# Which half of the array opens an item: fixed, or whichever is free

## The chip, the core and the metric

The kernel runs on one core of a Trainium2 chip. The time is device microseconds of one execution; what is compared is the median of several. TensorE (PE in the profile) multiplies, VectorE (DVE), ScalarE (ACT) and GpSimd (POOL) do the rest, and SyncE (SP) issues nearly all DMA transfers.

## The reference

Everything is float32, with 2048 tokens and a width of 512. The normalized input feeds two branches, and their results are multiplied.

```
xn = layernorm(x)
qkv = xn @ wqkv                       # 32 heads of 16
p = softmax(q k^T / 4, masked)        # each query sees the 256 latest keys
s = (p v) @ wo                        # 512 x 512
h = silu(xn @ w_gate) * (xn @ w_up)   # 512 x 1792 each
g = silu(h @ w_down)                  # 1792 x 512
out = x + s * g
```

## The kernel before

**Precision.** Matmuls run on float32r, a format that keeps fewer bits than float32. Each operand is therefore split into a high part (ACT copies it to float32r) and a low part (the difference, by POOL for weights and hidden activations, by DVE for others), and each product is three matmuls: high by high, high by low, low by high (`PAIRS`).

**Two halves.** PE is used as two arrays of 64 rows, `r` = 0 (lower, partitions 0 to 63) and 1 (upper, partitions 64 to 127). They work at the same time. A contraction over 128 rows is one matmul in each half, and both add into the same PSUM bank, but not at the same time: one half puts its whole share of the bank down first (it *opens* the item), then the other adds its own (it *closes* it). Between the two stands a handover, a DVE copy of one column (`ho`) on which the closing half waits. In this kernel the lower half always opens and the upper always closes, at least `LAG` = 7 matmuls later while the lower has work (`ready`).

**Units and items.** A unit is a block of weights and the work on it, an item one PSUM bank of output. Tokens are taken in four chunks of 512. `Proj` (profile name a) makes q and k of two groups of four heads, `Values` (vp) makes v, `GateUp` (g and u) a block of 128 hidden columns, `Down` (d) a quarter of the down product for 256 columns, `Wo` (s) the output projection for 256 columns. All have two items here. `dense_order` lists the units, `stream` their items. Four PSUM banks (`pf0` to `pf3`) serve the items, four others (`pr`) attention.

**Weights.** Unit n's lower half needs rows 0 to 63 of its weights at one time, and its upper half needs the others later. So blocks are shifted: block n holds the lower rows of unit n and the upper rows of unit n−1 (`block`, `units_of`). `w_fetch` loads a block by two DMAs of 64 partitions into one of two raw buffers (`wr`), `w_split` splits it on ACT (`wh`, line 429) and POOL (`wl`, line 434) into one of three pairs of buffers. Where the two units of a block differ in width, a piece of 64 partitions is split by itself. A block's buffers are free once the lower half has ended its unit and the upper the one before (`unit_end`).

**Attention** is laid between the dense matmuls. For each of 32 units of four heads (8 per chunk) PE makes the scores once for their row maxima (b, line 970; DVE reduces them into `m`), transposes the maxima (`mt`), ACT negates them (`ms`), and a DMA writes them as an extra row of q (`q<-ms`). Then PE makes the scores again with the maximum subtracted (c, line 1124), ACT takes the exponential into `p` (line 1085), POOL masks the diagonal blocks, and PE multiplies by v (pv, line 1161). q and k pass through DRAM (`qkd`): `Proj.done` stores them and `load_qk` loads them into the layout that attention needs.

**The order.** The program is written by a planner that runs while it is built. It keeps a clock for each half and each engine with costs in microseconds, and decides by these which half issues its next matmul (`next_mm`), what each engine's queue holds (`do`, `pump`) and when a DMA is issued (`dma`). On the chip each engine then takes its queue strictly in that order. Two of its assumptions matter below: `qk_at`, when q and k of an attention unit have landed, and `ms_at`, when the maxima have landed in q.

Of the kernel before, what the change touches and what calls it, by code (L numbers as in the profile page):

```python
# [41 lines left out]
LAG = 7  # L42
# [13 lines left out]
def tile_window_attention_swiglu_gate(  # L56
# [305 lines left out]
    def block(n, r):  # L362
        return n + r if n else 0

    class Unit:
# [3 lines left out]
        def wts(self, r):  # L369
            return wtile[block(self.n, r)]  # L370
# [10 lines left out]
    def units_of(j):  # L381
        return weighted.get(j), weighted.get(j - 1 if j else 0) if j != 1 else None

    def w_fetch(j):
        lo, up = units_of(j)
        if lo is None and up is None:
            return
        parts = [(r, u) for r, u in ((0, lo), (1, up)) if u is not None]
        box = []

        def go(r, u):
            if not box:
                if j == 2:
                    box.append(pers.tile([P, 1024], F32, name="wr2", tag=f"hr{NHID - 1}", bufs=1))
                else:
                    box.append(sb(f"wr{j}", [P, 1024], F32, "wr", 2))
            move(box[0][half(r), : u.width], u.src[half(r)])

        def then(t, last):
            if last:  # L400
                landed[j] = (t, box[0])
                w_split(j)

        for n, (r, u) in enumerate(parts):
            dma(now[0], lambda r=r, u=u: go(r, u), lambda t, n=n: then(t, n == len(parts) - 1),
                slack=1.0, kb=256 if j > 2 else 200)

    wpart = {}

    def w_split(j):  # L410
        if j not in landed or (j >= 3 and j - 3 not in ended_unit):
            return
        t, raw = landed.pop(j)
        t = max(t, ended_unit.get(j - 3, 0.0))
        w = [u.width if u else 0 for u in units_of(j)]
        hi, lo = [], []
        both = min(w)
# [6 lines left out]
        def high(pr, a, b):  # L424
# [4 lines left out]
            nc.scalar.activation(hi[0][pr, a:b], raw[pr, a:b], AF.Copy)  # L429

        def low(pr, a, b):
            if j == 0 and a == 0:
                nc.gpsimd.tensor_copy(spare, xt[0, list(normed)[-1][1]][:, :1])
            nc.gpsimd.tensor_tensor(lo[0][pr, a:b], raw[pr, a:b], f32(hi[0][pr, a:b]), op=ALU.subtract)  # L434
# [9 lines left out]
        def after_high(t, pr, a, b, sl):  # L444
            wpart[j, a, 0] = t
            do("G", t, 0.17 + 0.0021 * (b - a), lambda: low(pr, a, b), lambda t: done(t, a), sl, lambda: len(normed) >= 4)

        for n, (pr, a, b) in enumerate(cuts):
            sl = (0.0 if j >= 3 else 0.2) + 0.3 * n
            if j == n == 0:  # L450
                sl = -3.0
            do("S", t, 0.13 + 0.00078 * (b - a), lambda pr=pr, a=a, b=b: high(pr, a, b),
               lambda t, pr=pr, a=a, b=b, sl=sl: after_high(t, pr, a, b, sl), sl)

    half_ended = set()
# [56 lines left out]
    class Stationary(Unit):  # L514
# [6 lines left out]
        def inputs(self, i):  # L521
            if self.c == 0 and self.n == 0 and i == 0:
# [3 lines left out]
        def mms(self, i, r, pb):  # L526
            w = [t.rearrange("p (a k n) -> p a k n", a=2, k=KC) for t in self.wts(r)]
            xs = xn[self.c % 2]
            if self.c == 0 and self.n == 0 and i == 0:
                for a, b in ((0, 0), (1, 0), (0, 1)):  # L530
                    for part in range(2):
                        n = slice(256 * part, 256 * part + 256)
                        for k in range(KC):
                            def go(first, last, k=k, a=a, b=b, n=n):
                                return mm(pb[:, n], w[a][half(r), i, k, :], xs[b][half(r), k, n], first, last)
                            yield 256, go, lambda k=k, a=a, b=b, part=part: latest(
                                [(xlow if b else xhigh).get((k, part)), wpart.get((0, 0, a))]
# [116 lines left out]
    class Moving(Unit):  # L654
# [4 lines left out]
        def mms(self, i, r, pb):  # L659
            w = [t[:, : self.width].rearrange("p (k n) -> p k n", n=256) for t in self.wts(r)]  # L660
            for t in range(2):
# [833 lines left out]
```

## Time and profile before

| | us |
|---|---|
| median of 3 runs (868.84, 870.20, 873.62) | 870.2 |
| the profiled execution | 871.9 |
| its span, first to last instruction | 870.1 |
| PE busy | 856.9 |
| POOL busy | 606.2 |
| ACT busy | 505.3 |
| DVE busy | 484.0 |

The profile was taken of one execution, and its span is 1.8 us shorter than that execution's time. Busy times are unions: PE counts as busy when either half works. In the lists, a row of the timeline gives the start and the length in microseconds, the engine, the line, the operation, the names written and read, the shape and a count of rows merged into it; brackets give the idle time before it and what ended it. PEld are weight loads of PE, and a name with q (SPq, ACTq) is that engine's instruction queue. A matmul's shape, 64*128 64x512, is the rows and columns of its tile of the array, and then the moving operand.

### The profile page before, as it was taken

How to read it: one execution, taken by the hardware profiler on the slowest of the kernel's cores; microseconds unless marked ns; L12 is line 12 of the kernel's file. 1: busy time of each engine (PE TensorE's matmuls, PEld its weight loads, DVE VectorE, ACT ScalarE, POOL GpSimd, SP SyncE). 2: the span in 40 equal slices, each digit the busy share in tenths (PEclk: the TensorE clock that was granted, in tenths of full speed). 3: DMA queues.
4: the chain of work that ended last, by engine and by line, in shares of the span. 5: the costliest groups of instructions: out<-in, count | busy, mean ns of one | idle time of the engine just before them, and what ended most of it. 6: DMA issues, size and time to landing. Idle time of an engine off the chain costs nothing.

```text
span 870.1 us, 29847 instructions
## 1 busy us (share of the span) xinstructions
PE 856.9 (98%) x11960; PEld 790.0 (91%) x11960; DVE 484.0 (56%) x1627; ACT 505.3 (58%) x1074; POOL 606.2 (70%) x648
## 2 busy tenths in 40 slices
PE   9999999999999999999999999999999999999997
PEld 8799989998889898989989999898999989999897
DVE  4364456655646555766546766566555566554233
ACT  4355565555665567565577566665656865566532
POOL 6566565668786576666699686666658897759764
PEclk9999999999999999999999999999999999999999
DMA  5885855476877975655767997446657679643442
GB/s 140 191 195 118 229 116 156 119 174 168 193 156 185 253 185 115 137 150 125 179 160 192 225 211 189 115 150 139 178 131 183 159 172 209 170 130 112 108 123 77
DMA packets 69486, 139.60 MB, mean 160 GB/s; under 512 B 14546, under 2 KB 23250, under 8 KB 69348
## 3 DMA queue, kind: packets, MB, share of 16 engines
q1 hardware_dynamic: 69060, 137.18, 64.3%
q8 instruction: 94, 1.54, 0.8%
q10 hardware_dynamic: 288, 0.52, 0.2%
q14 instruction: 44, 0.36, 0.2%
HBM read 107.74 MB, written 29.62 MB: 158 GB/s over the span
## 4 chain that ended last, share of the span: by engine, by line
PE 80%; DMA 11%; POOL 4%; SPq 2%; issue 1%; ACT 1%; DVE 0%; ACTq 0%; POOLq 0%; DVEq 0%
PE d L470 16%; PE u L470 14%; PE g L470 14%; PE a L470 9%; PE pv L1161 7%; PE c L1124 5%; PE s L470 4%; PE vp L470 4%; PE b L970 4%; POOL wl L434 3%; DMA wr<-wgu 2%; SPq L95 2%; DMA q<-ms 1%; DMA r<-rd 1%; DMA wr<-wo 1%
## 5 line engine op out<-in xcount | busy, mean ns | idle before, releaser
L434 POOL TENSOR_TENSOR wl<-wr,wh 128x512 fp32r<-128x512 f32 (+2 forms) x258 | 306.7, 1208 | 117.0 <-ACT wh L429 111.0
L978 DVE CUSTOM_DVE_ANT_0 jk<-b,maskb 128x384 bf16<-128x384 f32 (+2 forms) x512 | 271.5, 530 | 140.6 <-PE b L970 69.4
L1085 ACT ACTIVATE p<-c 128x384 f32<-128x384 f32 (+1 forms) x480 | 208.2, 489 | 114.1 <-PE c L1124 97.6
L470 PE MATMUL d<-wh,hh 64*128 64x256 f32 x1792 | 259.3, 279 | 0.0
L470 PEld LDWEIGHTS d<-wh,hh 64*128 64x128 f32 x1792 | 225.6, 185 | 1.0 <-issue 0.6
L470 PE MATMUL d<-wl,hh 64*128 64x256 f32 x896 | 206.2, 279 | 0.0
L429 ACT ACTIVATE wh<-wr 128x512 fp32r<-128x512 f32 (+2 forms) x258 | 142.1, 593 | 57.3 <-DMA wr<-wgu 12.3
L470 PE MATMUL g<-xh,wh 64*128 64x512 f32 x448 | 169.7, 394 | 0.0
L470 PE MATMUL g<-xl,wh 64*128 64x512 f32 x448 | 169.1, 395 | 0.0
L470 PE MATMUL u<-xh,wh 64*128 64x512 f32 x448 | 169.1, 396 | 0.0
L470 PE MATMUL u<-xh,wl 64*128 64x512 f32 x448 | 168.9, 395 | 0.0
L470 PE MATMUL u<-xl,wh 64*128 64x512 f32 x448 | 168.4, 395 | 0.0
L470 PE MATMUL g<-xh,wl 64*128 64x512 f32 x448 | 168.2, 395 | 0.0
L470 PEld LDWEIGHTS d<-wl,hh 64*128 64x128 f32 x896 | 152.7, 185 | 0.4
L1098 POOL TENSOR_SCALAR_AFFINE_SELECT p<-p 128x512 f32<-128x512 f32 x128 | 81.4, 639 | 57.9 <-ACT p L1085 53.0
L970 PE MATMUL b<-k,q 48*128 48x384 f32 (+1 forms) x512 | 117.4, 334 | 2.4 <-DMA k<-qkd 1.5
L1124 PE MATMUL c<-q,k 49*128 49x384 f32 (+1 forms) x704 | 114.7, 306 | 3.9 <-ACT p L1085 2.7
L628 POOL TENSOR_TENSOR hh<-h,hh 128x512 fp32r<-128x512 f32 x56 | 72.7, 1298 | 46.8 <-ACT hh L624 41.2
L470 PE MATMUL a<-xh,wl 64*128 64x512 f32 (+1 forms) x264 | 96.8, 386 | 0.0
L470 PE MATMUL a<-xh,wh 64*128 64x512 f32 (+1 forms) x264 | 96.5, 390 | 0.0
L470 PE MATMUL a<-xl,wh 64*128 64x512 f32 (+1 forms) x264 | 95.4, 385 | 0.0
L1124 PEld LDWEIGHTS c<-q,k 49*128 49x128 f32 x704 | 85.4, 185 | 9.8 <-ACT p L1085 4.5
(102 smaller groups left out, 2100.5 us busy)
## 6 DMA issues: line engine op xcount, KB each, us to landing
wr<-wgu SPq DMA_DIRECT2D x112, 256.0 KB
k<-qkd SPq DMA_DIRECT2D x48, 192.0 KB
wr<-wqk SPq DMA_DIRECT2D x32, 256.0 KB
qkd<-qkh SPq DMA_DIRECT2D x32, 256.0 KB
qkd<-qkl SPq DMA_DIRECT2D x32, 256.0 KB
q<-qkd SPq DMA_DIRECT2D x64, 128.0 KB
wr<-wdn SPq DMA_DIRECT2D x32, 256.0 KB
od<-ev SPq DMA_DIRECT2D x32, 256.0 KB
```

The costliest lines, as they stand in the source:

```text
L95: eng.dma_start(dst, src)
L429: nc.scalar.activation(hi[0][pr, a:b], raw[pr, a:b], AF.Copy)
L434: nc.gpsimd.tensor_tensor(lo[0][pr, a:b], raw[pr, a:b], f32(hi[0][pr, a:b]), op=ALU.subtract)
L470: return nc.tensor.matmul(pb, a, b, start=first, stop=last, skip_group_check=True)
L628: nc.gpsimd.tensor_tensor(hl[:, 1, :], self.h, f32(hl[:, 0, :]), op=ALU.subtract)
L970: nc.tensor.matmul(pb[:, :w], qs[u % 3][r : r + 48, p, qb * P : (qb + 1) * P], ks[u % 3][r : r + 48, p, lo : lo + w], start=True, stop=True,)
L978: nc.vector.tensor_tensor_reduce(junk[:, :n], pb[:, :n], maskb[:, 3 * P - n :], 1.0, -3.0e38, ALU.add, ALU.max, m[:, col : col + 1],)
L1085: nc.scalar.activation(t[:, h, :], pc[:, a:b], AF.Exp, scale=DH ** -0.5)
L1098: nc.gpsimd.affine_select(s, s, [[0, 4], [1, P]], ALU.is_ge, 0.0, base=0, channel_multiplier=-1)
L1124: nc.tensor.matmul(pc[:, at0 : at0 + w], ks[u % 3][r : r + 49, p, k0 : k0 + P], qs[u % 3][r : r + 49, p, qb * P : qb * P + w], start=(i == ...
L1161: nc.tensor.matmul(pbs[r][0][32 * j : 32 * j + 32, q0:q1], vt[half(r), (4 * c + kb) % VT, VW * (4 * g + j) : VW * (4 * g + j) + 32], t[hal ...
```

## The change

A half that has finished its share of an item now chooses (`choice`): if an item that the other half opened has been handed over, it closes that one; otherwise it opens the next item of the stream, if a bank, the inputs and the weights are there. The fixed lag is gone. Because both halves now work on the same unit at about the same time, a block of weights is one unit's 128 rows, loaded by one DMA and split without pieces of 64 partitions; its buffers are free when both halves have ended all items of the unit (`item_end`). Counts replace the tests for the second item, since items can now close in any order. The first unit's second item may start on parts of its inputs as the first one does, and the high parts of both its pieces of weights are made first. The last unit (`Wo` of the last chunk, second half) has four items of 128 tokens in place of two of 256, with their own loads of x, products, additions and stores. Two assumptions of the planner move: q and k of the first attention unit land 2 us later, the maxima 2 us later (3.0 behind the transfer's planned end, before 1.0).

```diff
-LAG = 7
...
-    def block(n, r):
-        return n + r if n else 0
...
         def wts(self, r):
-            return wtile[block(self.n, r)]
+            return wtile[self.n]
...
     def w_fetch(j):
-        lo, up = units_of(j)
...
-        for n, (r, u) in enumerate(parts):
-            dma(now[0], lambda r=r, u=u: go(r, u), lambda t, n=n: then(t, n == len(parts) - 1),
-                slack=1.0, kb=256 if j > 2 else 200)
+        u = weighted.get(j)
...
+            move(t[:, : u.width], u.src)
...
+        dma(now[0], go, then, slack=1.0, kb=512 if j > 2 else 400)
...
-        cuts = [(slice(0, P), a, min(a + 512, both)) for a in range(0, both, 512)]
-        if max(w) > both:
-            r = 0 if w[0] > both else 1
-            cuts += [(half(r), a, min(a + 512, max(w))) for a in range(both, max(w), 512)]
+        cuts = [(a, min(a + 512, w)) for a in range(0, w, 512)]
...
-            if j == n == 0:
-                sl = -3.0
+            if j == 0:
+                sl = -3.0 + 0.1 * n
...
-    def unit_end(j, t):
-        if (0, j) in half_ended and (1, max(j - 1, 0)) in half_ended:
+    def item_end(j, t):
+        item_ended[j] = item_ended.get(j, 0) + 1
+        if item_ended[j] == 2 * weighted[j].items:
             ended_unit[j] = t
             w_split(j + 3)
...
-            if self.c == 0 and self.n == 0 and i == 0:
+            if self.c == 0 and self.n == 0 and i == r:
...
             self.src = wo[hf]
+            if c == NCH - 1 and hf == 1:
+                self.items = 4
...
-                qk_at[u] = t
+                qk_at[u] = t + (0.0 if u else 2.0)
...
-            dma(t, put, lambda t: ms_at.__setitem__(u, t + 1.0), -3.0, 8)
+            dma(t, put, lambda t: ms_at.__setitem__(u, t + 3.0), -3.0, 8)
...
+    def choice(r):
+        t = max(clock[r], now[0])
+        for n in half_done[r]:
+            if handed.get(n, 1e9) <= t:
+                return n, False
+        n = opened[0]
+        if n < len(stream):
+            u, i = stream[n]
+            w = wpart.get((0, 512 * i, 0)) if u.n == 0 else wready.get(u.n)
+            w = latest([bank_time(fb_free), u.inputs(i), w])
+            if w is not None and w <= t:
+                return n, True
+        return None
...
-        lag = ended[pos[1]] + (LAG * MM if pos[1] else 0.0)
-        t0 = None if pos[0] == len(stream) else ready(0)
-        return max(t, lag) if t0 is not None and t0 <= now[0] else t
+        return None if choice(r) is None else 0.0
```

Three places show what moves. The first is PE's queue at the first dense item. The names are the PSUM bank written (a0_0 and a0_1 are the two items of the first `Proj`), the activations (xh, xl) and the weights (wh, wl, the number behind them is the block's); a bank's name read in turn with another's means the two halves in turn. Before:

```order
L470 MATMUL a0_0_218<-xh0_79,wh0_199 128x256 x8
L470 MATMUL a0_0_218<-xh0_79,wl0_200 128x256 x8
L470 MATMUL a0_0_218<-xl0_80,wh0_199 128x256 x8
L470 MATMUL a0_1_262<-xh0_79,wh0_199 128x512
L470 MATMUL a0_1_262<-xl0_80,wh0_199 128x512
L470 MATMUL a0_1_262<-xh0_79,wl0_200 128x512
L470 MATMUL a0_0_218<-xh0_79,wh0_199 128x256 x2
L470 MATMUL a0_1_262<-xh0_79,wh0_199 128x512
```

And in the changed kernel, the end of the same stretch (the rows ahead of these alternate likewise from the first matmul on):

```order
L451 MATMUL a0_0_216<-xl0_80,wh0_193 128x256
L451 MATMUL a0_1_218<-xl0_80,wh0_193 128x256
L451 MATMUL a0_0_216<-xh0_79,wh0_193 128x512
L451 MATMUL a0_0_216<-xl0_80,wh0_193 128x512
L451 MATMUL a0_1_218<-xh0_79,wh0_193 128x512
L451 MATMUL a0_1_218<-xl0_80,wh0_193 128x512
```

Before, 24 matmuls of the lower half stand alone at the head of the queue, and the upper half's first comes behind three of the next item. Now the lower half opens a0_0 while the upper opens a0_1, and each closes the other's.

The second place is the end of PE's queue, the last matmuls of the last unit (s3_1_0 and so on are its items). Before, from the last matmul of the lower half on (s3_1_1 with block 119):

```order
L470 MATMUL s3_1_1_17107<-wh119_16844,xl0_80 128x256
L470 MATMUL s3_1_0_17050<-wh120_16931,xh0_79 128x256
L470 MATMUL s3_1_0_17050<-wl120_16932,xh0_79 128x256
L470 MATMUL s3_1_0_17050<-wh120_16931,xl0_80 128x256
L470 MATMUL s3_1_0_17050<-wh120_16931,xh0_79 128x256
```

This goes on with s3_1_0 and then s3_1_1, 39 rows in all behind the lower half's last. Now the last ten rows are these:

```order
L451 MATMUL s3_1_2_16977<-wh119_16782,xh0_79 128x256
L451 MATMUL s3_1_3_16989<-wh119_16782,xl0_80 128x256
L451 MATMUL s3_1_2_16977<-wl119_16783,xh0_79 128x256
L451 MATMUL s3_1_3_16989<-wh119_16782,xh0_79 128x256
L451 MATMUL s3_1_2_16977<-wh119_16782,xl0_80 128x256
L451 MATMUL s3_1_3_16989<-wl119_16783,xh0_79 128x256
L451 MATMUL s3_1_3_16989<-wh119_16782,xl0_80 128x256
```

After the last row shown, three more of s3_1_3 follow. The halves take turns nearly to the end.

The third is SP's queue at the first loads of q and k (`qkd` read) and the weights ahead of them. Before:

```order
L95 DMA qkd<-qkh_0_319 8x16x512
L95 DMA wr_330<-wqk 64x1024
L95 DMA wr_330<-wgu 64x1024
L95 DMA qkd<-qkl_0_320 8x16x512
L95 DMA qkd<-qkh_1_359 8x16x512
L95 DMA qkd<-qkl_1_360 8x16x512
L95 DMA wr_408<-wgu 64x1024
L95 DMA wr_408<-wqk 64x1024
L95 DMA q_72<-qkd 32x2x512
```

Now:

```order
L94 DMA wr_321<-wqk 128x1024
L94 DMA qkd<-qkh_0_326 8x16x512
L94 DMA qkd<-qkh_1_337 8x16x512
L94 DMA qkd<-qkl_0_327 8x16x512
L94 DMA qkd<-qkl_1_338 8x16x512
L94 DMA wr_409<-wgu 128x1024
L94 DMA q_72<-qkd 32x2x512
```

A load of weights is one row of 128 partitions in place of two rows of 64, each from another unit, and fewer of them stand ahead of the first load of q.

More of the change, by code (lines that the diff above doesn't have):

```diff
@@ L1332, in next_mm @@
                     u.begin(i)
[L1333 to L1334 removed]
+            else:
+                half_done[r].remove(n)
+            run[r] = [list(u.mms(i, r, banks[n])), 0, n, opens]
+        todo, m, n, opens = run[r]
+        u, i = stream[n]
         cols, go = todo[m][:2]
[L1336 removed]
+        go(opens and m == 0, not opens and m == len(todo) - 1)
         issue(r, cols)
[L1338 removed]
+        if r == 0:
             work[0] += cols * MM / 512
```

159 lines of the change are left out of this document (67 added, 92 removed).

## The prediction

> **What bounds the kernel now.** I read the page's busy times first, then its chain that ended last, then the timeline at both ends, then the list of waits of PE and of its weight loads.
>
> ```profile
> PE 856.9 (98%) x11960; PEld 790.0 (91%) x11960; DVE 484.0 (56%) x1627; ACT 505.3 (58%) x1074; POOL 606.2 (70%) x648
> ...
> PE 80%; DMA 11%; POOL 4%; SPq 2%; issue 1%; ACT 1%; DVE 0%; ACTq 0%; POOLq 0%; DVEq 0%
> ```
>
> PE is the engine that sets the time, and no other is near it. But "98% busy" hides something: the array runs as two halves of 64 rows, and PE counts as busy when only one of them works. The timeline shows the pace of two working halves.
>
> ```profile
> 20.26 0.39 PE L470 MATMUL a<-xl,wh 64*128 64x512 f32 x1
> 20.37 0.39 PE L470 MATMUL u<-xh,wh 64*128 64x512 f32 x1
> 20.49 0.39 PE L470 MATMUL a<-xh,wl 64*128 64x512 f32 x1
> 20.60 0.40 PE L470 MATMUL u<-xl,wh 64*128 64x512 f32 x1
> ```
>
> The upper half (a) starts a 512-column matmul every 0.23 us, and so does the lower (u), in between. A matmul alone goes no faster (the 35 steps from 861.00 to 865.12 below take 0.118 us each, for 256 columns), so each microsecond in which one half has nothing costs half a microsecond of work, and the end is set by the half that finishes last. Both halves carry the same work. At the ends they are not level:
>
> ```profile
> 10.90 2.20 PE L470 MATMUL a<-xh,wh 64*128 64x256 f32 x8
> ...
> 13.25 6.30 POOL L434 TENSOR_TENSOR wl<-wr,wh 128x512 fp32r<-128x512 f32 x5 [1.63 <-ACT wh L429]
> ...
> 14.78 0.39 PE L470 MATMUL a<-xh,wh 64*128 64x512 f32 x1
> ...
> 14.97 0.15 DVE L467 COPY ho<-a 80x1 f32<-80x1 f32 x1 [1.55 <-PE a L470]
> ...
> 15.19 0.39 PE L470 MATMUL a<-xh,wh 64*128 64x256 f32 x1
> ```
>
> ```profile
> 860.88 0.28 PE L470 MATMUL s<-wh,xl 64*128 64x256 f32 x2
> 861.00 0.28 PE L470 MATMUL s<-wh,xh 64*128 64x256 f32 x1
> ...
> 865.12 0.28 PE L470 MATMUL s<-wh,xl 64*128 64x256 f32 x1
> ```
>
> ```profile
> 865.50 0.69 DVE L822 SCALAR_TENSOR_TENSOR y<-gp,s 128x512 f32<-128x512 f32 x1 [1.43 <-PE s L470]
> 866.23 0.69 DVE L829 TENSOR_TENSOR y<-y,xr 128x512 f32<-128x512 f32 x1
> ```
>
> The lower half opens a0_0 at 10.90; the first matmul of the upper is the 256-column one at 15.19 (at 14.78 it is the lower half's next item), 4.3 us later. The skew stays through the program: both end a matmul pair at 860.88, and from 861.00 on the rows read x1. That is the upper half alone, 4.2 us long. Behind it come a product, an addition and the last store.
>
> In the middle, both halves stand still at few places, and the waits name them:
>
> ```profile
> PE c L1124 <- ACT p L1085: 2.7, 4, 1.0
> PE b L970 <- DMA k<-qkd: 1.5, 1, 1.5
> PE c L1124 <- DMA q<-ms: 1.3, 3, 0.8
> ```
>
> ```profile
> PEld c L1124 <- ACT p L1085: 4.5, 7, 1.4
> ...
> PEld c L1124 <- DVE ho L467: 1.6, 2, 1.2
> ```
>
> **The change, part by part.** The sum is made against the profiled execution's own 871.9 us (a span of 870.1 and 1.8 around it).
>
> *The skew.* In the order of the changed kernel both halves open an item at the start (a0_0 and a0_1), and at the end only the last four matmuls are one half's alone. So the 4.2 us at the end go: **−4.2**. The start needs the second piece of the first weights earlier; its ACT split is now queued ahead of the eight xh pieces, and POOL had room for it (its second split began only at 13.25, after 1.63 idle), so I cost that at nothing; if it delays xh it costs at most its 0.6.
>
> *Pauses of one half.* With two free choices the halves also get out of step. I counted it in the two orders, row by row, each matmul at the interval above (0.23 for 512 columns, less in proportion), with no waits: before, the lower half stands still for 3.9 us in the whole program; after, the lower for 6.8 and the upper for 6.6. **+2.7**, between 0 (a pause may coincide with a stall that is there anyway) and 4.
>
> *The first attention block.* Planned landings of the first q and k are 2 us later in the changed planner.
>
> ```profile
> 36.48 0.28 PE L970 MATMUL b<-k,q 48*128 48x256 f32 x1
> ...
> 38.25 0.47 PE L970 MATMUL b<-k,q 48*128 48x256 f32 x3 [1.48 <-DMA k<-qkd]
> ```
>
> Between these two rows neither half starts anything: 1.8 us. The changed order has 6 more dense matmuls of the lower half ahead of the first b and 22 more of the upper, so b comes later and a0_0, from which q and k are loaded, is closed earlier. The stall goes: **−1.8**, between 0 and −2.
>
> *The maxima's way to q.* The planner now expects them 2 us later, so c comes later behind its transpose.
>
> ```profile
> 716.57 7.11 DMA q<-ms
> ...
> 723.82 0.50 PE c L1124 x4
> ```
>
> Here PE waited for that transfer. The waits put down to it come to 1.3, and the 1.6 put down to the handover (which had long been done) look the same in place. I take **−2.0**, between 0 and −2.9. What comes later in exchange is the softmax, which has slack, since the last visit of attention ends at 815 and dense work runs on to 865:
>
> ```profile
> 812.79 2.38 PE pv L1161 x93
> ```
>
> *One load of weights in place of two.* 240 loads of 64 partitions become 120 of 128 with the same bytes.
>
> ```profile
> L95 SPq DMA_DIRECT2D wr<-wgu x112: 465/582/1579, 6.5 to 810.4; - x112
> ```
>
> ```profile
> ACT wh L429 <- DMA wr<-wgu: 12.3, 7, 3.2
> ACT wh L429 <- DMA wr<-wo: 4.7, 2, 3.2
> ACT wh L429 <- DMA wr<-wqk: 4.0, 1, 4.0
> ACT wh L429 <- DMA wr<-wv: 2.8, 1, 2.8
> ```
>
> ```profile
> 285.06 7.54 DMA wr<-wgu
> ...
> 292.70 1.15 ACT wh L429 x2
> 293.86 0.55 ACT p L1085 x2
> ...
> 294.45 0.51 PE c L1124 x4
> ```
>
> The third fence shows how a late load reaches PE: ACT takes its queue in order, stands at wh until the load lands, the exponentials p queue behind it, and c waits for a PSUM bank that p frees. Eleven such waits hold ACT for 23.8 us; of PE's time 7.2 (2.7 + 4.5) follow. One issue less brings each load 0.58 us nearer. 11 × 0.58 = 6.4 of 23.8, so about a quarter of the 7.2: **−2.0**, between 0 and −7.2.
>
> *Costs: handovers.* The closing half may start only after a DVE copy has read the bank (0.15 us, the row at 14.97). The longest crowd in front of it on DVE are the 512 reductions:
>
> ```profile
> L978 DVE CUSTOM_DVE_ANT_0 jk<-b,maskb 128x384 bf16<-128x384 f32 (+2 forms) x512 | 271.5, 530 | 140.6 <-PE b L970 69.4
> ```
>
> Before, the closer starts at least seven matmuls (1.6 us) after the opener's end in all items but the first. After, by the same count, 45 of 242 have under 1 us, 6 under 0.5. From the end of the opener's last issue (14.78) to the closer's first matmul (15.19) is 0.41, so a free DVE still meets nearly all. PE takes its queue in order, too: in the fence at 36.48 dense matmuls of both halves stand behind the waiting b, and none starts. So a late handover stops both halves. A DVE that is busy 56% of the time with pieces of 0.53 is late by 0.56 × 0.53 / 2 = 0.15 on average; were none of it covered, 45 × 0.15 = 6.7. Most have 0.2 to 0.6 to spare: **+0.8**, from 0 to 6.7.
>
> The Trainium skill (TensorE: Matmul & The Clock Gate, "The mechanism") speaks against the change here: matmuls start in strict queue order, also between tiles of the array. The trace agrees, by the 1.8 us in which both halves stood. If a waiting half left the other free, the 0.8 would be 0.4 and the sum 0.4 less.
>
> *Costs: weight buffers.* A unit's block is now read from the first opening to the second closing. Counted in the order, it lives 11.6 us in the median, before 8.2, and there are still three. From the last read of block k−3 to the first of block k there are under 6 us for 32 blocks, least 4.0; before, for one, and the rest have over 8.6. The split takes:
>
> ```profile
> 35.19 1.16 ACT L429 ACTIVATE wh<-wr 128x512 fp32r<-128x512 f32 x2 [3.97 <-DMA wr<-wqk]
> ...
> 35.90 2.50 POOL L434 TENSOR_TENSOR wl<-wr,wh 128x512 fp32r<-128x512 f32 x2 [5.09 <-ACT wh L429]
> ```
>
> 35.19 to 38.40 is 3.2 us, so it fits under 4.0 if both queues are free, and the cover that hid it (5 us and more) is gone. A mask ahead of it costs 0.63:
>
> ```profile
> 709.61 0.63 POOL L1098 TENSOR_SCALAR_AFFINE_SELECT p<-p 128x512 f32<-128x512 f32 x1
> ```
>
> From 0 to 32 × 0.63 = 20; I take **+1.5**, near the unobstructed row. *PSUM banks* are reopened sooner too (47 within 3 us of their closing, before 16), against an eviction of one or two operations of 0.6 to 0.7: **+0.4**, from 0 to 3.
>
> *The last unit in four items.* After the last matmul DVE had two operations of 0.69; the new order leaves one product and three additions of half the size, 4 × 0.35: nothing won. The last store is half as long: **−0.2**, between 0 and −0.5. Its two more loads of x and two more stores pass SP while it has nothing else to issue but stores. *POOL and ACT* lose 18 of their 258 splits, all of half height; neither is the bound, so that is worth nothing by itself.
>
> The sum: −4.2 + 2.7 − 1.8 − 2.0 − 2.0 + 0.8 + 1.5 + 0.4 − 0.2 = −4.8, to 867.1 for the profiled execution. That one stands 1.7 above the median of the three runs (870.2), so the median goes to **865.4**.
>
> **The rivals.**
>
> *Gains go back* (0.36): the skew is won but the pauses cost the full 4, and late loads and maxima stall PE as before. Only the 1.8 of the first block and some tenths stay: 868.5. For it: PE's stalls are spread, and those that a shift removes tend to return elsewhere. Against: the largest single ones have causes that the change addresses.
>
> *Slower, by just-in-time weights* (0.16): the 32 splits with under 6 us come late by half a microsecond each, because POOL (70% busy) has a mask or a hidden-activation split ahead. 32 × 0.5 = 16 in place of 1.5, so +9.7: 880. From a mean of 0.2 us on (32 × 0.2 = 6.4) the gain is used up. Against: the smallest spacing, 4.0, is still over 3.2.
>
> *Loads land in time* (0.11): the merged loads come early enough that no wh waits for one. Then all 7.2 go rather than 2.0: 860.
>
> The Trainium skill (SBUF — State Buffer, "Can I just issue two DMAs to hit both halves?") gives a reason for it: two loads to partition halves serialize, each reaching 8 of 16 ports. By its asymptotes (218 and 436 GB/s) the pair takes an estimated 2.4 us and the single one 1.2. No trace of before has a weight load of 128 partitions to compare.
>
> *That the change does nothing it says* I rule out: both orders show the two openings, the single loads and the four last items.
>
> **How the numbers follow.** Forecast 0.37, loads in time 0.11, gains back 0.36, slower 0.16. A measurement of this kernel tells 0.5% (4.4 us) from no change. The first two lie beyond it: faster 0.48, same 0.36, slower 0.16. The range runs from 860 less its own tenths, 859, to 875, which takes in gains given back in full and the milder half of the slower case.
>
> **What would show it.** Right: the first upper matmul within 0.5 us of the lower at 11; rows x1 at the end for under 1 us; no wait of b for k<-qkd; c waiting for q<-ms nowhere; fewer waits of wh for wr. Wrong: PE or its loads waiting for POOL wl (weights just in time), for DVE ho (handovers), or more time in which PE is not busy than the 13.2 us of now (870.1 − 856.9). The most likely error is in the costs of the buffers, which rest on counts in the order and not on a row.

## The result, and the profile after

The changed kernel takes **864.0 us** (median of 5 runs, 863.57 to 865.33) against 870.2: a ratio of 0.9926, with a 95% interval of 0.9899 to 0.9952. The forecast was 865.4, in a range of 859 to 875. The profiled execution took 865.33, with a span of 863.6.

The page's busy times and the shares of its chain that ended last, after the change:

```profile
PE 854.2 (99%) x11960; PEld 785.1 (91%) x11960; DVE 486.2 (56%) x1633; ACT 495.7 (57%) x1056; POOL 595.9 (69%) x630
...
PE 94%; DMA 3%; DVE 1%; ACT 1%; issue 0%; SPq 0%; POOL 0%; DVEq 0%; POOLq 0%; ACTq 0%
```

PE's share of the chain rises from 80% to 94%, and DMA's falls from 11% to 3%. The timeline after, at the start and at the end (start and length in us, engine, line, operation, count):

```profile
10.94 2.37 PE L451 MATMUL a<-xh,wh 64*128 64x256 f32 x16
...
15.16 0.22 DVE L448 COPY ho<-a 80x1 f32<-80x1 f32 x2 [1.50 <-PE a L451]
...
15.37 0.57 PE L451 MATMUL a<-xh,wh 64*128 64x512 f32 x2 [0.24 <-DVE ho L448]
...
858.16 0.28 PE L451 MATMUL s<-wh,xh 64*128 64x256 f32 x1
...
858.74 0.28 PE L451 MATMUL s<-wh,xl 64*128 64x256 f32 x1
859.13 0.42 DVE L813 SCALAR_TENSOR_TENSOR y<-gp,s 128x256 f32<-128x256 f32 x1 [0.16 <-PE s L451]
859.47 1.09 DVE L820 TENSOR_TENSOR y<-y,xr 128x256 f32<-128x256 f32 x3
```

At the start x16 stands where x8 stood: both halves open at 10.94, and both pay for a handover at 15.16, since they end their first items together. At the end one half is alone from 858.16 to 858.74; before, for 4.2 us. The chain of DVE behind the last matmul is as long as before: one product and three additions end at 860.56, 1.8 us after the last matmul's start.

What PE and its weight loads wait for, and the one kind of wait left of ACT's `wh` for a load of weights, after:

```profile
PE b L961 <- ACT p L1076: 2.0, 2, 1.3
...
PE c L1115 <- ACT p L1076: 0.7, 1, 0.7
PE a L451 <- DVE ho L448: 0.2, 1, 0.2
...
PEld b L961 <- ACT p L1076: 3.2, 4, 1.7
...
PEld c L1115 <- ACT p L1076: 1.6, 4, 1.1
...
ACT wh L413 <- DMA wr<-wgu: 3.2, 3, 1.7
```

The waits for `k<-qkd` and `q<-ms` are gone. Neither list has a wait for `wl`, so no weights came just in time, and `wh` waits 3.2 us for loads where it waited 24.6 (the prediction's 23.8, and 0.8 more for `wdn`). All five signs that the prediction named for being right are there, and PE is idle for 9.4 us (863.6 − 854.2) where it was for 13.2.

The two lists are not to be added. Where PE waits, its load of weights waits too, for the same thing, and both end together: the wait of b that is 1.3 us long in PE's list ends at 227.56, and so does the one of 1.7 in that of the loads.

**An account of the 6 us.** As for the prediction, I walked through PE's order without waits: each matmul takes the interval of its width (0.23 us for 512 columns), the two halves run beside each other, and no row starts before the row ahead of it. The walk contains the skew and the pauses, and it is an estimate. What the trace takes beyond it, between the first dense matmul and the end of the last, I call the rest: waits, and time at a lower clock.

| kernel (one profiled run) | trace | walk | rest |
|---|---|---|---|
| before | 854.3 | 833.1 | 21.2 |
| after | 847.9 | 831.7 | 16.2 |
| after, profiled a second time | 846.3 | 831.7 | 14.6 |

The walk gives 1.4 and the rest 5.0 to 6.6. A second count of the same two orders, with attention's matmuls priced otherwise, gives 2.0 in place of 1.4, so the walk is good to some half a microsecond. The rest is nearly all waits: those of PE's loads, from the first dense matmul on, add up to 22.0, 17.4 and 15.9 us in the three profiles. The prediction had 1.5 (−4.2 + 2.7) and 3.1, so the question is what else left the rest.

### The profile page after: what moved, and what is told of

It is laid out like the page before. It is cut to its first block, busy times and chain, and to the rows that moved or that the text cites. A ratio compares the mean times of both kernels' runs of the same rounds, so it can differ in the third digit from the quotient of the medians.

```text
span 863.6 us, 29615 instructions
## 1 busy us (share of the span) xinstructions
PE 854.2 (99%) x11960; PEld 785.1 (91%) x11960; DVE 486.2 (56%) x1633; ACT 495.7 (57%) x1056; POOL 595.9 (69%) x630
## 3 DMA queue, kind: packets, MB, share of 16 engines
q1 hardware_dynamic: 67204, 137.17, 57.3%
## 4 chain that ended last, share of the span: by engine, by line
PE 94%; DMA 3%; DVE 1%; ACT 1%; issue 0%; SPq 0%; POOL 0%; DVEq 0%; POOLq 0%; ACTq 0%
PE u L451 18%; PE d L451 18%; PE g L451 18%; PE a L451 11%; PE pv L1152 8%; PE c L1115 5%; PE s L451 5%; PE vp L451 5%; PE b L961 5%; DMA r<-rd 1%; DMA wr<-wgu 1%; DVE jk L969 0%; DMA xt<-x 0%; PE xp L469 0%; ACT wh L413 0%
## 5 line engine op out<-in xcount | busy, mean ns | idle before, releaser
L418 POOL TENSOR_TENSOR wl<-wr,wh 128x512 fp32r<-128x512 f32 x240 | 296.7, 1259 | 166.0 <-ACT wh L413 146.9
L451 PE MATMUL d<-wh,hh 64*128 64x256 f32 x1792 | 236.7, 278 | 0.0
L451 PEld LDWEIGHTS d<-wh,hh 64*128 64x128 f32 x1792 | 208.7, 185 | 1.4 <-issue 0.8
L451 PE MATMUL d<-wl,hh 64*128 64x256 f32 x896 | 191.7, 279 | 0.0
L413 ACT ACTIVATE wh<-wr 128x512 fp32r<-128x512 f32 x240 | 136.4, 616 | 69.1 <-issue 15.6
L451 PEld LDWEIGHTS d<-wl,hh 64*128 64x128 f32 x896 | 143.1, 185 | 0.4
L1115 PE MATMUL c<-q,k 49*128 49x384 f32 (+1 forms) x704 | 106.2, 305 | 0.7 <-ACT p L1076 0.7
L451 PE MATMUL a<-xh,wl 64*128 64x512 f32 (+1 forms) x264 | 86.8, 386 | 0.0
L451 PEld LDWEIGHTS g<-xh,wl 64*128 64x128 f32 x448 | 82.3, 186 | 3.0
L451 PEld LDWEIGHTS g<-xl,wh 64*128 64x128 f32 x448 | 82.0, 185 | 3.1 <-issue 0.2
```

The lines of the kernel that those rows point to most:

```text
L413: nc.scalar.activation(hi[0][:, a:b], raw[j][:, a:b], AF.Copy)
L418: nc.gpsimd.tensor_tensor(lo[0][:, a:b], raw[j][:, a:b], f32(hi[0][:, a:b]), op=ALU.subtract)
L451: return nc.tensor.matmul(pb, a, b, start=first, stop=last, skip_group_check=True)
L1115: nc.tensor.matmul(pc[:, at0 : at0 + w], ks[u % 3][r : r + 49, p, k0 : k0 + P], qs[u % 3][r : r + 49, p, qb * P : qb * P + w], start=(i == ...
```

## The experiments

Twelve kernels ran in three sittings, each beside the kernel before (medians 870.18, 868.65 and 870.08). The changed kernel itself ran again in the first sitting alone, with 864.14. In the second, the kernel with two loads of 128 partitions, which has the same order, took 863.95, so 864.1 is used beside all three. PE's order is that of the changed kernel, row for row, in the runs of the first table.

### One load or two, and what late work costs

The changed kernel as it is (no edit):

> The changed kernel as it is, for the same chip and the same rounds as the three beside it. All theories: 0.990 to 0.995 of the kernel before, about 6 us less (864 against 870).

Two loads of 64 partitions:

```diff
-            move(t[:, : u.width], u.src)
+            move(t[half(0), : u.width], u.src[half(0)])
+            move(t[half(1), : u.width], u.src[half(1)])
```

> The changed kernel, with each block of weights loaded by two DMAs of 64 partitions again, issued one behind the other; nothing else moves, PE's order is the same row for row. Theory A (the merged load is worth what the prediction gave it: ACT stands at wh for a late load, the exponentials queue behind it, PE follows): 2 us slower than the changed kernel, waits of ACT wh for the loads up from 3.2 us in 3 to over 10. Rival B (all of PE's 7.2 us behind ACT came from late loads, and the pair takes twice as long): 5 to 7 us slower. Rival C (a weight load now lands long before its buffer is free, and wh waits for the buffer, not for the load; fewer waits for loads came from the new order, not from the merged load): within 0.5 us of the changed kernel, and the waits of wh for the loads stay under 6 us.

Two loads of 128 partitions (run in the second sitting):

```diff
-            move(t[:, : u.width], u.src)
+            move(t[:, :512], u.src[:, :512])
+            move(t[:, 512 : u.width], u.src[:, 512:])
```

> The changed kernel, with each block of weights loaded by two DMAs of 128 partitions and half the columns, issued one behind the other; PE's order is the same row for row. Beside the run with two loads of 64 partitions (3.7 us slower than the changed kernel) it tells the partition halves from the mere number of loads. Theory A (the loss came from the second issue on SP and a later landing, of whatever shape): 3 to 4 us slower, issues of 0.5 us and more each. Rival B (it came from the 64 partitions: the issue of 0.58 in place of 0.35 and the slower transfer): within 1 us, issues near 0.35, DMA share of the loads' queue near 58%.

Later splits:

```diff
+            if j >= 3 and a == 0:
+                nc.gpsimd.tensor_tensor(lo[0][:, :256], raw[j][:, :256], f32(hi[0][:, :256]), op=ALU.subtract)
             nc.gpsimd.tensor_tensor(lo[0][:, a:b], raw[j][:, a:b], f32(hi[0][:, a:b]), op=ALU.subtract)
```

> The changed kernel, with one more subtraction of 128x256 (about 0.65 us) on POOL ahead of the first wl piece of each block from the fourth on, which the planner does not know of; PE's order is the same row for row. It makes every split later by what the rival of just-in-time weights feared. Theory A (the blocks have cover: in the trace of the changed kernel 6 of 117 blocks have under 0.65 us from the end of the split to the first use, short by 2.2 us together): 1 to 3 us slower. Rival B (the 32 blocks that are reopened within 6 us all come late by it): 32 x 0.65 = 21 us slower. Rival C (POOL's masks and hidden-activation splits wait behind it, and PE waits for those instead): 3 to 8 us slower, with new waits of pv for POOL p or of dense rows for POOL.

Later handovers:

```diff
-        nc.vector.tensor_copy(pers.tile([MW, 1], F32, name="ho", tag=ring("ho", 2), bufs=1), pb[:MW, 0:1])
+        h = pers.tile([MW, 1], F32, name="ho", tag=ring("ho", 2), bufs=1)
+        for _ in range(3):
+            nc.vector.tensor_copy(h, pb[:MW, 0:1])
```

> The changed kernel, with each handover's copy made three times in place of once, so that the closing half may start 0.3 us later (two more copies of 0.15); PE's order is the same row for row. Theory A (handovers have the margin that the trace shows: 17 of 242 closings start under 0.3 us behind their copy, short by 2.2 us together): 1 to 2.5 us slower. Rival B (none of it is covered, a late closing stops both halves, for PE takes its queue in order): 45 closings with under 1 us x 0.3 = 13 us slower. Rival C (one half's wait is filled by the other): under 0.5 us.

| run | median us | ratio to before, 95% | rest |
|---|---|---|---|
| changed kernel | 864.14 | 0.9932 (0.9909 to 0.9954) | 14.6 |
| two loads of 64 partitions | 867.88 | 0.9968 (0.9945 to 0.9991) | 19.2 |
| two loads of 128 partitions | 863.95 | 0.9935 (0.9912 to 0.9957) | 15.4 |
| later splits | 871.77 | 1.0017 (0.9997 to 1.0037) | 22.6 |
| later handovers | 885.62 | 1.0177 (1.0148 to 1.0206) | 36.4 |

**Loads.** Theory A had the mechanism and about half the size: two loads of 64 partitions cost 3.7 us. ACT's waits for loads in that run, then the timeline of ACT and that of PE around one late load:

```profile
ACT wh L414 <- DMA wr<-wgu: 12.7, 9, 2.1
...
ACT wh L414 <- DMA wr<-wdn: 1.9, 1, 1.9
```

```profile
299.41 1.15 ACT L414 ACTIVATE wh<-wr 128x512 fp32r<-128x512 f32 x2 [1.91 <-DMA wr<-wdn]
300.46 1.07 ACT L1077 ACTIVATE p<-c 128x512 f32<-128x512 f32 x2
```

```profile
299.76 0.39 PE L452 MATMUL u<-xl,wh 64*128 64x512 f32 x1
301.58 0.44 PE L1116 MATMUL c<-q,k 49*128 49x384 f32 x2 [1.43 <-ACT p L1077]
301.86 0.39 PE L452 MATMUL u<-xh,wl 64*128 64x512 f32 x1
```

ACT stands 1.91 us at `wh`; the exponentials `p` queue behind it; c waits 1.43 for a bank that `p` frees; and the dense rows u and g behind c start nothing either. The waits for loads are back at 14.6 us. PE's loads wait 7.3 us for `p` in that run and 3.4 in the changed kernel beside it, and the 3.9 between them is about the 3.7 that the run costs.

The two loads of 128 partitions cost nothing, so it isn't the number of loads. The issue of the `wgu` blocks on SP (shortest, median and longest in ns, first and last start in us), for single loads, for halves of partitions and for halves of columns:

```profile
L94 SPq DMA_DIRECT2D wr<-wgu x56: 328/352/1227, 6.4 to 801.6; - x56
```

```profile
L94 SPq DMA_DIRECT2D wr<-wgu x112: 465/584/2572, 7.9 to 805.4; - x112
```

```profile
L94 SPq DMA_DIRECT2D wr<-wgu x112: 323/423/1977, 6.9 to 801.2; - x112
```

An issue takes 0.58 us in the median for 64 partitions, and 0.35 to 0.42 for 128. The loads' queue is busy 64.5% of the 16 engines' time with halves of partitions, 58.1% with halves of columns and 57.3 to 58.4% with single loads, for the same 137 MB. The Trainium skill (SBUF — State Buffer, "Can I just issue two DMAs to hit both halves?") says that only one transfer spanning all 128 partitions reaches all ports. The runs agree: split by columns, the pair is free (−0.2 us), and split by partitions it costs 3.7.

**Splits.** The split of each block 0.65 us later costs 7.6 us, by rival C. Waits of weight loads in that run:

```profile
PEld pv L1154 <- POOL p L1095: 10.5, 19, 1.2
...
PEld u L453 <- POOL wl L420: 0.5, 1, 0.5
```

PE waits for `wl` once. What comes late are the masks of `p`, which queue behind the splits on POOL. So the weights have cover, as theory A says, but POOL's queue has not, and the cost passes through another product of that engine than the one I feared for.

**Handovers.** 0.3 us more in each handover costs 21.5 us; all three expectations missed, the highest by 8.5. Waits of PE, then of its loads:

```profile
PE mt L997 <- DVE ho L450: 1.3, 5, 0.4
...
PE a L453 <- DVE ho L450: 0.6, 1, 0.6
...
PEld mt L997 <- DVE ho L450: 9.2, 24, 0.7
...
PEld c L1117 <- DVE m L971: 2.2, 9, 0.4
...
PEld a L453 <- DVE ho L450: 1.4, 3, 0.8
```

Two things were not in my count. The transposed maxima (`mt`) are handed over too, 32 times, and 24 of these hold PE's loads for 0.4 us each. And 548 more copies keep DVE busy 562 us in place of 486, so that the row maxima `m` come late as well. The run therefore doesn't price the 242 dense handovers by themselves: the lists give them 5.1 us of PE's loads, and the rest isn't told apart. It does show that there is little cover under a handover.

### The parts of the change that alter the order

The upper half closes only, seven matmuls behind (core of the edit):

```diff
         for n in half_done[r]:
-            if handed.get(n, 1e9) <= t:
+            lag = ended[n] + (7 * MM if n and choice(0) else 0.0)
+            if max(lag, handed.get(n, 1e9)) <= t:
                 return n, False
+        if r:
+            return None
```

> The changed kernel, with the lower half opening every item and the upper closing it, seven matmuls behind, as before the change; the single loads, the planned landings and the four last items stay. Theory A (the free choice wins the skew of 4.2 us and loses some of it to pauses of one half): 1 to 3 us slower than the changed kernel, with the upper half's first matmul over 3 us behind the lower's and the rows x1 at the end back for 3 to 4 us. Rival B (the pauses cost nothing, since the halves stood at those places anyway): 3.5 to 4.5 us slower. Rival C (the free choice is worth nothing, or less, and the merged loads carry the gain): within 1 us.

Two items in the last unit:

```diff
-            if c == NCH - 1 and hf == 1:
-                self.items = 4
```

> The changed kernel, with the last unit in two items in place of four; PE's order differs in its last 44 rows alone. Theory A (the prediction): 0 to 0.5 us slower, since the chain behind the last matmul is then two operations of 0.69 in place of one of 0.42 and three of 0.36, and the last store is twice as long. Rival B (with larger items one half is alone for longer at the end): 1 to 2 us slower, rows x1 at the end for over 1.5 us.

Both planned landings as before:

```diff
-                qk_at[u] = t + (0.0 if u else 2.0)
+                qk_at[u] = t
...
-            dma(t, put, lambda t: ms_at.__setitem__(u, t + 3.0), -3.0, 8)
+            dma(t, put, lambda t: ms_at.__setitem__(u, t + 1.0), -3.0, 8)
```

> The changed kernel, with the two planned landings (first q and k, maxima) as before the change; the planner then orders the rest anew, so rows differ through the whole program. Theory A (the prediction: the first block's stall of 1.8 us and the maxima's 2.0 come back): 3 to 4 us slower, waits of b for k<-qkd and of c for q<-ms over 2 us together. Rival B (opening with both halves moved b behind the transfer by itself, and only the maxima need the constant): 1 to 2 us slower, no wait of b for k<-qkd. Rival C (neither constant matters): within 1 us, neither wait back.

The second of these two edits alone:

> The changed kernel with the planned landing of the maxima as before the change, that of the first q and k left 2 us later. With both as before it was 4.8 us faster than the changed kernel, and its waits for ACT p were gone. Theory A (the later maxima crowd the exponentials on ACT, and c and b wait for the banks): 4 to 5 us faster, PE and its loads waiting under 1.5 us for ACT p. Rival B (the first block's landing did it): within 1 us of the changed kernel, the waits for ACT p still 4 us and more together.

The reverse, in the kernel before (both landings 2 us later, nothing else):

> The kernel before, with the two planned landings alone as in the change (first q and k 2 us later, maxima 2 us later); lower half first, two loads, all else as before. Theory A (the prediction: 1.8 and 2.0 us of stalls go): 3 to 4 us faster than the kernel before, no wait of b for k<-qkd or of c for q<-ms. Rival B (in the changed kernel the old landings were 4.8 us faster, so a later landing costs more than the stall that it removes): 2 to 5 us slower. Rival C (the waits go and others take their place): within 1 us, with more waits for ACT p.

An edit without meaning:

```diff
-LEAD = 1.1
+LEAD = 1.11
```

> The changed kernel with a meaningless edit: the planner's lead of attention work, 1.1 us, becomes 1.11. It moves as many of PE's rows as the old landings do, and no margin. It tells how far an order that is merely another one moves the time. Theory A (an order alone is worth under 1.5 us, so the 4.8 us of the old landings have a cause): within 1.5 us of the changed kernel. Rival B (orders differ by several us by chance): 2 to 5 us off, on either side, with the waits for ACT p changed by as much.

And on top of the old landings, an earlier addition in the last unit:

```diff
-            do("V" if last else "G", t, 0.61 if last else 1.24, add, after_add, 2.0,
+            do("V" if last else "G", t, 0.61 if last else 1.24, add, after_add, -1.0 if last and hf else 2.0,
```

> The changed kernel with both planned landings as before the change (859.3 us), and in the last unit each addition of x set ahead of the next item's product on DVE, so that behind the last matmul stand two operations of 128x256 in place of three or four; only the last dozen rows of PE move. Theory A (the chain behind the last matmul counts in full): 0.3 to 0.8 us faster than with the old landings alone. Rival B (the last store waits for its queue or its issue all the same): no difference over 0.2 us.

| run | median us | ratio to before, 95% | granted clock, profiled run | walk | rest |
|---|---|---|---|---|---|
| lower half opens all | 869.46 | 1.0008 (0.9983 to 1.0034) | 0.990 | 838.0 | 18.9 |
| last unit in two items | 866.73 | 0.9971 (0.9949 to 0.9994) | 0.999 | 833.5 | 15.7 |
| old landings | 859.31 | 0.9876 (0.9845 to 0.9906) | 1.000 | 832.2 | 10.2 |
| old landing of the maxima | 859.74 | 0.9881 (0.9856 to 0.9906) | 0.999 | 832.6 | 10.4 |
| kernel before, later landings | 873.92 | 1.0045 (1.0023 to 1.0068) | 0.997 | 836.9 | 18.3 |
| lead 1.11 | 868.31 | 0.9983 (0.9966 to 1.0000) | 0.996 | 831.8 | 18.9 |
| old landings, early additions | 859.62 | 0.9881 (0.9856 to 0.9906) | 1.000 | 832.2 | 9.9 |

**The meaningless edit** goes first, since it is the measure for the others: it costs 4.2 us, the size that rival B gave it. The means are not rival B's, though: PE's loads wait 4.2 us for ACT p, against 3.4. Four fifths of the cost is one place. The same stretch in windows, of the run with lead 1.11 and of that with the old landing of the maxima (window, its length, then the busy time of PE, PEld, DVE, ACT and POOL with their instructions, the granted clock, DMA share, GB/s):

```profile
264.00:266.00 2.00, 2.00 (x16) 1.53 (x12) 1.86 (x6) 1.76 (x5) 2.00 (x2) 1.00 0.26 76
266.00:268.00 2.00, 1.23 (x7) 0.68 (x6) 1.86 (x6) 1.84 (x5) 2.00 (x4) 1.00 0.47 126
...
269.00:270.00 1.00, 0.73 (x3) 0.28 (x1) 0.86 (x4) 1.00 (x4) 1.00 (x3) 0.50 1.00 246
...
272.00:274.00 2.00, 1.90 (x13) 1.40 (x14) 1.54 (x6) 1.51 (x4) 2.00 (x3) 0.50 0.63 215
274.00:276.00 2.00, 2.00 (x24) 2.00 (x23) 0.00 (x0) 0.24 (x1) 1.94 (x4) 0.54 0.98 377
```

```profile
266.00:268.00 2.00, 2.00 (x29) 1.92 (x27) 1.86 (x6) 1.46 (x4) 2.00 (x3) 1.00 0.44 57
...
272.00:274.00 2.00, 2.00 (x36) 2.00 (x34) 1.39 (x8) 0.73 (x3) 0.47 (x1) 1.00 0.88 267
```

With lead 1.11 the dense work runs dry at 265, and PE has only b and c, 7 matmuls in 2 us in place of 29. From 269.0 to 275.8 the clock is granted at half: 6.8 × 0.5 = 3.4 us. In the changed kernel's own trace no window between the first and the last matmul shows this. Without the clock, then, the edit moved 0.8 us.

**Free choice.** With the lower half opening all, the clock halves twice (rows of that run, at the start and in the same place as above):

```profile
16.00:18.00 2.00, 2.00 (x14) 1.90 (x15) 0.15 (x1) 0.00 (x0) 2.00 (x3) 0.50 0.47 137
...
276.00:280.00 4.00, 4.00 (x24) 4.00 (x25) 1.25 (x5) 0.49 (x2) 0.60 (x2) 0.50 0.77 222
```

Its median, 5.3 us above the changed kernel's, lies beyond all three expectations. Its 12 runs follow their granted clock: 874.1 at 0.989, 868.5 at 0.995, 865.4 at 1.000. In its one run at the full clock it is 1.4 us slower than the changed kernel (864.0 at 0.999 and 1.000), which is theory A's 1 to 3; by that run the other 3.9 of the medians' 5.3 are clock. Its walk is 6.3 us longer. In the profiled run the clock is at half for 6.8 us from 14.4 and for 10.2 from 273.9, a loss of 8.5, and the rest without it is only 10.4: where the order holds a pause, a wait finds its place in it, and the two don't add up.

**Four items.** Two items cost 2.6 us, more than theory A or rival B gave them, and the rows show rival B's mechanism:

```profile
854.49 0.28 PE L451 MATMUL s<-wl,xh 64*128 64x256 f32 x1
...
856.37 0.28 PE L451 MATMUL s<-wh,xl 64*128 64x256 f32 x1
856.89 0.38 PE L451 MATMUL s<-wh,xh 64*128 64x256 f32 x1 [0.24 <-DVE ho L448]
...
859.71 0.28 PE L451 MATMUL s<-wh,xl 64*128 64x256 f32 x1
860.10 0.69 DVE L811 SCALAR_TENSOR_TENSOR y<-gp,s 128x512 f32<-128x512 f32 x1 [3.25 <-PE s L451]
```

One half opens the last item alone until 856.37, then the other closes it alone until 859.71: 5.2 us in which one half works, against 0.6 with four items. The skew is only won at the end because the last items are small.

**Planned landings.** With both as before, the changed kernel is 4.8 us *faster*, against all three expectations, and 4.4 with the maxima's alone. Neither run has a wait of b for `k<-qkd` or of c for `q<-ms`. What is gone are the waits for ACT p: none is left of PE, 0.2 us of its loads, where the changed kernel has 2.7 and 4.8 (1.1 and 3.4 in its second profile). The largest of them stand behind a late load. The first three rows are of the changed kernel, the last two of the run with the old maxima, at the same block of weights:

```profile
225.98 1.15 ACT L413 ACTIVATE wh<-wr 128x512 fp32r<-128x512 f32 x2 [1.70 <-DMA wr<-wgu]
227.04 0.85 ACT L1076 ACTIVATE p<-c 128x384 f32<-128x384 f32 x2
...
227.56 0.44 PE L961 MATMUL b<-k,q 48*128 48x384 f32 x1 [1.31 <-ACT p L1076]
```

```profile
223.77 1.14 ACT L413 ACTIVATE wh<-wr 128x512 fp32r<-128x512 f32 x2
224.82 0.85 ACT L1076 ACTIVATE p<-c 128x384 f32<-128x384 f32 x2
```

That is the path of the two loads once more: ACT waits for a load, `p` queues behind it, PE waits for `p`. With the old maxima the load has landed in time. In the kernel before, the later landings cost 3.8 us, as rival B has it, and a wait for the maxima stays all the same:

```profile
PE c L1124 <- DVE m L978: 1.9, 2, 1.7
PE c L1124 <- DMA q<-ms: 1.5, 2, 1.1
```

The first block's wait goes there, the walk is 3.8 longer, and the clock is at half from 244.7 to 248.1. So the later landing of the maxima doesn't do what it was credited with in either kernel.

Whether the old one is better by a mechanism, or leads to an order in which that load happens to land in time, isn't settled. The two runs with the old maxima share most of their order, and the test of theory A (waits for ACT p under 1.5) came out as expected, but a late load passes it as well as exponentials that crowd ACT. The edit without meaning moved 4.2 us, but neither of these two runs loses the clock that made most of it; as another order alone it moved 0.8, and one such order is no measure of how far others go.

**Early additions** make no difference (859.62 and 859.31): the last two products became ready together, and the last two additions follow them as before.

## Why the prediction was right, and where it was not

The time was right within 1.4 us, the sign too, and the account shows which terms carried it.

- **Skew and pauses (−4.2 + 2.7): right.** The walk gives −1.4 to −2.0. Both ends look as forecast: both halves open at 10.94, and rows x1 last 0.6 us at the end. With the lower half opening all, the kernel is 1.4 us slower in its one run at the full clock.
- **The first block (−1.8): the stall went, by one of the two causes named.** It went without the planned landing too, as the run with old landings shows; the order in which both halves open is enough.
- **The maxima (−2.0): the step that failed.** The waits went, but I put that down to the planner's 2 us. With the old constant they don't return in the changed kernel, and with the new one they stay in the kernel before. By the traces the transfer itself varies. In the kernel before, the three blocks that waited started c 5.0, 7.3 and 6.4 us behind the end of the transfer's issue, and others started 4.5 behind without a wait; with the later constant one block still waits until 8.7. With the old constant the changed kernel starts c 5.2 us behind at the least, and none waits. Why its transfers land in time isn't shown. A likely reason is SP's queue, in which a block's loads now take 0.35 us rather than two times 0.58, but that was only argued. The size was right for the wrong reason too: 1.3 of PE and 1.6 of its loads are in the main the same two stalls, 1.9 us in all, so the 2.9 at the end of the range was never there.
- **One load in place of two (−2.0): right mechanism, mis-sized.** Taken back alone in the changed kernel, it measured 3.7, within the range of 0 to 7.2. I counted one issue less (0.58); a block's load is 0.82 nearer by SP alone (1.17 − 0.35), and the transfer of all partitions is quicker, which I had only as a rival. The 7.2 from which the term was taken counts stalls twice: each of c's four waits of PE (2.7) ends together with one of the seven of its loads (4.5). So 4.5 us could go, and 1.2 more at b, which I left out; the rival in which all loads land in time promised too much.
- **Handovers (+0.8): right for this order, for a thin reason.** The one wait of a dense row for `ho` in the trace is 0.4 us of PE's loads (PE's own 0.2 is the same one), at a, where both halves end their first items together. The dose of 0.3 us shows how near the edge that is. The rule of strict queue order (the Trainium skill, TensorE: Matmul & The Clock Gate, "The mechanism"), weighed in the prediction, fits the rows of the run with two loads, where neither half starts anything from 299.76 to 301.58 while c waits.
- **Weight buffers (+1.5): nothing of it.** PE never waited for `wl`. The rival of just-in-time weights had the right dose and the wrong victim: 0.65 us a split costs 7.6 us, through the masks.
- **PSUM banks (+0.4)** were not tested by themselves.
- **Four last items (−0.2): mis-sized.** I looked only behind the last matmul, where indeed nothing is won; their worth is the 2.6 us of evenness before it, which I had booked under the skew.
- **Missing: the granted clock.** 74 runs of the kernel before have a median of 869.5. The 23 with a granted clock of 0.999 and more have 867.8, the 23 with 0.996 and less 871.0. None of 13 runs of the changed kernel is under 0.998. So of the 6 us some 1.7 is likely clock that the kernel before loses in some of its runs. That is read from the runs together; the profiled one shows no such stretch, and at 0.999 and more the kernel before still spreads from 865.5 to 873.3, which stays unexplained.

Together, by the waits of PE's loads in the profiles: the wait for the first k (1.7) goes, those for the maxima (1.9) go, and those for ACT p fall from 5.7 to 4.8 in one profile of the changed kernel and to 3.4 in the other. With the walk's 1.4 that is 5.9 and 7.3 us, and the traces show 6.4 and 8.0. So the gains came about as large as forecast (7.5 in all, with the last unit's 0.2), and of the 2.7 that it feared for handovers, weights and banks hardly anything shows. That the time came within 1.4 us has some luck in it: one gain came by another way than the one named, one was taken from a sum that counts twice, and the clock was left out. These terms are read beside each other in two different orders; the runs that take a part back show that parts don't simply add up.

The best version that ran is the change with the old landings, 859.3 us: 1.2% under the kernel before (0.9845 to 0.9906).

## What to carry to other kernels

Load a block with one DMA over all partitions; here two halves by partitions cost the issuing queue and the transfer alike, and the loss showed on PE by way of what queued behind the waiting consumer. Where a list of waits has an engine and its loads apart, see whether both rows end at the same time before adding them. A queue's margin is found by adding a known delay without moving anything else, and it may turn up in another product of that engine than the one in mind. Where a planner lays out the whole program, run an edit without meaning first: an effect of another edit that is no larger says little, and the granted clock by windows tells how much of it is mere clock.

## What the runs showed of the hardware

**The clock halves without PE standing still.** From 266 to 268, ahead of the drop at 269.0, PE is busy 1.23 of 2.00 us, and its longest idle time is 0.77 us; it is the number of matmuls that is low. With the lower half opening all, the clock is at half from 14.4 to 21.3, though PE reads busy throughout: only one half of the array had been working since 11.08. The kernel before starts with one half alone as well, and its profiled run keeps the full clock, so not every such stretch brings a drop. Counted from the traces' matmuls (an estimate: 0.23 us of one half for 512 columns), the two halves together did 18, 25, 31 and 37% of what they can in the 3.4 us ahead of the four drops. Anywhere else between the start and the last matmuls the least is 34% (the kernel before, at its first attention block) and 36% (its start); in the changed kernel it is 46%, further from the edge. The four stretches at half clock last 3.4, 6.8, 6.8 and 10.2 us, one, two, two and three times 3.4. The Trainium skill (TensorE: Matmul & The Clock Gate, "What's actually happening") gives a free-running window of 3413 ns, and these lengths agree. The same page's "HAM oscillation — how this bites in real kernels" warns of idle gaps over about 3.4 us. Here the longest gap close ahead of a drop is 1.7 us, in the kernel before with later landings, and ahead of the others 0.8 and less, so in this kernel the clock fell without such a gap.

**The issue of a load took longer over fewer partitions**, not with more bytes: 0.58 us in the median for 64 partitions (256 KB), 0.42 for 128 partitions (256 KB) and 0.35 for 128 partitions (512 KB).
